# Banded attention ahead of a cosine MLP: value rows of four heads at 192 bytes in a scratch tensor, one load per half batch, for pairs 4 to 7 as well

## Chip, core and metric

One Trainium2 chip, one of its cores. The metric is the device time of one execution in microseconds (us), the median of three runs. All profile times are microseconds from the start of the profiled span unless a number is marked ns.

## What is computed

Attention over 8 batches of 8 heads with 576 positions of width 64, and after it an MLP whose activation is h·cos(h). A query sees keys at most 32 positions away; eight global positions see all and are seen by all.

```python
scores = scale * np.matmul(q, k.transpose(0, 1, 3, 2))
mask = (np.abs(pos[:, None] - pos[None, :]) <= 32) | is_global[:, None] | is_global[None, :]
attn = softmax(np.where(mask, scores, -1e9))
x = np.matmul(attn, v).transpose(0, 2, 1, 3).reshape(4608, 512)
h = x @ w_in            # 512 -> 2048
out = (h * np.cos(h)) @ w_out
```

## The kernel before

**Pieces of work.** The heads are taken in 32 pairs, four pairs to a batch, two pairs to a "half batch" (16 half batches, called s). For one pair the keys are cut into 11 blocks of 56 queries against 120 keys, and the 8 global rows are put in front of each block, so that a block is 128 keys (tile `kw`), 64 queries (tile `qb`) and 128 value rows (tile `vw`). The steps of a pair are:

- `k`, `q` (`local_k` L495, `local_q` L504): fill `kw` and `qb`. For pairs 0 to 7 this is 32 transposes on TensorE (L492) with one copy of `kw` on ScalarE (L499) and two copies of `qb` (L512), from tiles `kn` and `qn` that GpSimd's queue loads with a cast (`load_qk`, L269, step `L`). From pair 8 on, k and q are first cast to scratch tensors `k16` and `q16` in device memory (`cast_half`, L253, steps `K` and, inside the loop, `G`), then read back with a transposing transfer (`turn_half` L272) and copied by VectorE (L502, L515).
- `s` (`scores`, L517): 11 matmuls in three groups, exp on ScalarE (L527), the mask on VectorE (L528).
- `p` (`values`, L531): 22 matmuls with `vw`, then sums, reciprocals and the scaling on VectorE (L542 to L548).
- `x` (`turn_x`, L552): six transposes, two VectorE operations; after the fourth pair of a batch, eight GpSimd copies (L568) that put the global columns in place. They use eight indices that GpSimd reads into registers (`pool_idx`).

**Where value rows come from.** For pairs 0 to 7 (half batches 0 to 3) the values are loaded in natural order by 24 transfers on SyncE's queue (`load_vn`, L334), cast to 16 bits by one ScalarE and two VectorE instructions per half batch (`cast_vn`, L346, step `C`) and moved to the right partitions by matmuls with shift matrices (`spread`, L361, step `w`: 32 matmuls of 128 columns at L370 and L374, then two ScalarE and one VectorE evacuations at L377 per pair). From pair 8 on, v is cast to `v16` (row after row of 64 elements, 128 bytes) and each pair's `vw` is filled from it by two to five transfers on SyncE's queue (`load_v` L305), in pieces of 128 bytes; two more bring the global rows (`load_vg` L379).

**The MLP.** Work goes in tiles of 512 tokens. One unit of the first product is `mlp_in` (four matmuls of 512 columns, L578) with `mlp_act` (sine table on ScalarE L584, product on VectorE L585); one unit of the second product is `mlp_out` (four matmuls, L595; after each fourth, an evacuation and an output transfer, L604). The weights come by GpSimd's queue with a cast: `w_in` in four quarters (`W`, L688), `w_out` in one transfer (`O`, L692).

**The order** is written out by hand. `FRONT` runs all steps of pairs 0 to 7 except the first scores' preparations; `MID`, `FOURTH`, `FIFTH`, `SIXTH` and `ORDER` are the bodies for half batches s = 3, 4, 5, 6 and later ones, in which `1` is a unit of the first product, `2` one of the second, `m` and `t` the matmul part and the activation part of a `1`. Each engine and each queue works its instructions in this order. At the end of a body `bring(s + 2)` (step `B`) turns k and q of the half batch after next and loads its values; in the middle `G` (`casts`) issues the casts of half batch s + 3 on GpSimd's queue. The step `A` (`later_rows`) is 24 small transfers on SyncE's queue for the global rows of batches 4 to 7. The first 20 units of the first product are spread over `FRONT` (2) and `MID` (18); then come the first units `2`, at the start of `FOURTH`.

Of the kernel before, what the change touches and what calls it, by code (L numbers as in the profile page):

```python
# [19 lines left out]
P = 128  # L20
NP = H // 2
# [21 lines left out]
MID = "+ 1 1 kc qc 1 1 kd qd V K6 1 1 1 1 1 1 B5 1 1 n2 1 1 1 1 1 1 -"  # L43

FOURTH = "2 2 sa0 sa1 sa2 2 sz0 2 sz1 sz2 pa 1 1 2 xa pz G 1 1 2 xz n 1 1 2 kc qc 1 kd qd 2 1"
# [5 lines left out]
FRONT = ("s0.0 s0.1 s0.2 k1 q1 C0 w0 s1.0 s1.1 s1.2 L2 p0 k2 q2 C1 w1 x0 s2.0 s2.1 s2.2 W0 p1 k3 q3 C2 w2 x1 "  # L51
         "s3.0 s3.1 s3.2 L3 W1 A g4 g5 p2 k4 q4 w3 x2 s4.0 s4.1 s4.2 g6 g7 c4 K4 W2 W3 p3 k5 q5 C3 w4 x3 s5.0 s5.1 s5.2 p4 k6 q6 w5 x4 n0 "
         "s6.0 s6.1 s6.2 K5 p5 k7 q7 w6 x5 B4 s7.0 s7.1 s7.2 O p6 w7 n1 x6 m p7 m x7 t t")
# [145 lines left out]
def kernel(  # L199
# [38 lines left out]
    v16 = dram.tile([B * H * S, D], FP16)  # L238
# [4 lines left out]
    NV = 4  # L243
    kT = [keep.tile([P, 2, KT], FP16, name=f"kT{i}") for i in range(2)]
    qT = [keep.tile([P, 2, QT], FP16, name=f"qT{i}") for i in range(2)]
    kn = [keep.tile([KP, 2 * 2, RW, D], FP16, name=f"kn{i}") for i in range(2)]
    qn = [keep.tile([QP, 2 * 2, RW, D], FP16, name=f"qn{i}") for i in range(2)]
    vw = [keep.tile([P, NB, 2, D + 1], FP16, name=f"vw{i}") for i in range(NV)]
# [4 lines left out]
    def cast_half(s, which):  # L253

        base = s * 4 * S * D
        for x in which:
            if x == "v":
                nc.gpsimd.dma_start(v16[s * 4 * S : (s + 1) * 4 * S].rearrange("(n r) d -> n (r d)", r=16),
                                    dview(v, base, (16 * D, 4 * S // 16), (1, 16 * D)))
            else:  # L260
                src, dst = {"k": (k, k16), "q": (q, q16)}[x]
                nc.gpsimd.dma_start(dst[s].rearrange("t (h d) -> t h d", h=4),  # L262
                                    dview(src, base, (D, S), (S * D, 4), (1, D)))
# [41 lines left out]
    def load_v(pr):  # L305


        b, h0 = pr // NP, 2 * (pr % NP)
        vt = vw[pr % NV]
        for h in range(2):  # L310
            lo, i0, i1 = (b * H + h0 + h) * S * D, 0, NB
            if pr == 4 * SB and h == 0:
                nc.sync.dma_start(vt[G + 32 : P, 0, h, 0:D], dview(v16, lo, (D, W - 32), (1, D)))
                i0 = 1
# [304 lines left out]
    def weight_squares(c, j):  # L619
        if j == 0:  # L620
            w_sq[c] = work.tile([P, NC, 512], FP16, tag="wsq", bufs=1, name="wsq")
# [243 lines left out]
```

## Time and profile before

| What | Value |
|---|---|
| three runs, us | 366.85, 370.04, 370.23 (median 370.04) |
| profiled execution, us | 371.58, of which the span is 369.8 |
| busy: TensorE, VectorE, ScalarE, GpSimd | 335.9, 266.3, 249.5, 105.9 us |
| TensorE idle in 24.9 to 87.95 us (front and `MID`) | about 10 us |
| TensorE idle in 138 to 282 us | 0 |
| first matmul of the second product (`FOURTH`) | 87.8 us |
| SyncE: the 24 transfers of step `A` | 27.78 to 46.98 us |
| `w_out` issued | 51.68 us |

How to read it: the span falls into a front (to about 72 us), in which attention of pairs 0 to 7 is most of the work and TensorE, VectorE and ScalarE take turns; a middle, in which TensorE never stops; and a tail, in which only the MLP is left. Time that an engine other than TensorE saves in the middle is worth nothing, and time that TensorE spends waiting in the front shifts everything after it.

### The profile page before, as it was taken

How to read it: one execution, taken by the hardware profiler on the slowest of the kernel's cores; microseconds unless marked ns; L12 is line 12 of the kernel's file. 1: busy time of each engine (PE TensorE's matmuls, PEld its weight loads, DVE VectorE, ACT ScalarE, POOL GpSimd, SP SyncE). 2: the span in 40 equal slices, each digit the busy share in tenths (PEclk: the TensorE clock that was granted, in tenths of full speed). 3: DMA queues.
4: the chain of work that ended last, by engine and by line, in shares of the span. 5: the costliest groups of instructions: out<-in, count | busy, mean ns of one | idle time of the engine just before them, and what ended most of it. 6: DMA issues, size and time to landing. Idle time of an engine off the chain costs nothing.

```text
span 369.8 us, 8014 instructions
## 1 busy us (share of the span) xinstructions
PE 335.9 (91%) x2934; PEld 184.9 (50%) x2934; DVE 266.3 (72%) x615; ACT 249.5 (67%) x384; POOL 105.9 (29%) x239
## 2 busy tenths in 40 slices
PE   0399883999998999999999999999999999999992
PEld 0277673545553545555555555555555444444441
DVE  7659974696888888888888888888878445455410
ACT  5488882679776677778777868677787756644300
POOL 6735670161335250705253252603000100000000
PEclk9999997899999999999999999999999999999999
DMA  5979999999999999999999999999920000100111
GB/s 92 197 129 159 180 165 107 198 176 147 102 161 105 194 126 195 125 169 138 195 161 159 160 142 165 160 202 118 130 59 31 28 30 28 57 30 28 53 64 65
DMA packets 176280, 45.57 MB, mean 123 GB/s; under 512 B 164937, under 2 KB 171337, under 8 KB 176041
## 3 DMA queue, kind: packets, MB, share of 16 engines
q1 hardware_dynamic: 112601, 27.61, 58.3%
q0 software_dynamic: 63632, 17.37, 50.3%
q8 instruction: 25, 0.41, 0.5%
q14 instruction: 22, 0.18, 0.2%
HBM read 45.07 MB, written 20.05 MB: 176 GB/s over the span
## 4 chain that ended last, share of the span: by engine, by line
PE 79%; DVE 6%; issue 5%; ACT 3%; POOL 3%; DMA 2%; POOLq 0%; ACTq 0%
PE po L595 32%; PE ph L578 30%; PE st L525 5%; PE pv L537 4%; PE tx L560 2%; PE t L374 2%; DMA qn<-in_q_dram 2%; DVE g L585 2%; ACT e L527 1%; PE t L370 1%; PE t L492 1%; PE pn L628 1%; DVE xn L548 1%; POOL q L262 1%; ACT qb L512 1%
## 5 line engine op out<-in xcount | busy, mean ns | idle before, releaser
L584 ACT ACTIVATE cos<-ph,pio 128x512 f16<-128x512 f32 x144 | 97.1, 687 | 66.3 <-PE ph L578 64.7
L595 PE MATMUL po<-w_out,g 128*128 128x512 f16 x576 | 141.6, 379 | 0.0
L578 PE MATMUL ph<-xT,w_in 128*128 128x512 f16 x576 | 140.1, 379 | 0.3 <-DVE g L585 0.2
L585 DVE TENSOR_TENSOR g<-cos,ph 128x512 f16<-128x512 f16 x144 | 95.9, 685 | 46.9 <-ACT cos L584 44.9
L595 PEld LDWEIGHTS <-g 128*128 128x128 f16 x576 | 55.2, 98 | 62.1
L578 PEld LDWEIGHTS <-w_in 128*128 128x128 f16 x576 | 53.6, 98 | 60.5 <-issue 1.3
L527 ACT ACTIVATE e<-st 128x512 f16<-128x512 f32 (+1 forms) x96 | 47.9, 561 | 15.5 <-PE st L525 9.4
L528 DVE TENSOR_TENSOR pm<-e,mask 128x512 f16<-128x512 f16 (+1 forms) x96 | 37.2, 405 | 22.8 <-ACT e L527 21.0
L752 POOL COPY gate<-xn 1x1 f16<-1x1 f16 x12 | 2.2, 181 | 132.3 <-DVE xn L548 132.3
L525 PE MATMUL st<-qb,kw 128*128 128x128 f16 x352 | 29.2, 223 | 9.4 <-issue 5.0
L525 PEld LDWEIGHTS <-kw 128*128 128x128 f16 x352 | 24.1, 100 | 19.8 <-issue 9.1
L548 DVE TENSOR_TENSOR xn<-pv,r_all 128x768 f16<-128x768 f32 x32 | 30.7, 958 | 1.7
L568 POOL COPY xT<-xg 128x4 f16 x64 | 19.6, 306 | 28.7 <-DVE xT L563 25.3
L262 POOL DMA_DIRECT2D q<-in_q_dram x12 | 26.2, 2181 | 0.0
L614 ACT ACTIVATE sq<-xn 128x1536 f16<-128x1536 f16 x16 | 23.6, 1476 | 0.0
L515 DVE COPY qb<-qT 64x616 f16<-64x616 f16 x48 | 22.1, 460 | 0.3
L374 PE MATMUL t<-xT 112*128 112x128 f16 (+1 forms) x168 | 21.1, 240 | 0.7 <-ACT xT L349 0.4
L600 ACT COPY o<-po 128x512 f32<-128x512 f32 x18 | 10.5, 586 | 15.5 <-PE po L595 15.1
L262 POOL DMA_DIRECT2D k<-in_k_dram x12 | 19.8, 1646 | 0.0
L370 PE MATMUL t<-vg,xT 128*128 128x128 f16 x88 | 18.4, 242 | 0.9 <-issue 0.6
L537 PE MATMUL pv<-vw,pm 128*64 128x65 f16 x704 | 18.5, 199 | 0.0
L602 DVE COPY o<-po 128x512 f32<-128x512 f32 x18 | 12.3, 685 | 6.9 <-PE po L595 6.9
(123 smaller groups left out, 326.8 us busy)
## 6 DMA issues: line engine op xcount, KB each, us to landing
out_dram<-o SPq DMA_DIRECT2D x36, 256.0 KB
vw<-v SPq DMA_DIRECT2D x35, 165.0 KB
v<-in_v_dram POOLq DMA_DIRECT2D x12, 288.0 KB, 4.3
k<-in_k_dram POOLq DMA_DIRECT2D x12, 288.0 KB, 9.2
q<-in_q_dram POOLq DMA_DIRECT2D x12, 288.0 KB, 15.8
vn<-in_v_dram SPq DMA_DIRECT2D x20, 112.0 KB
w_in<-in_moe_w_in_dram POOLq DMA_DIRECT2D x4, 512.0 KB, 12.3
w_out<-in_moe_w_out_dram POOLq DMA_DIRECT2D x1, 2048.0 KB
```

Source lines behind the costliest of these rows:

```text
L262: nc.gpsimd.dma_start(dst[s].rearrange("t (h d) -> t h d", h=4), dview(src, base, (D, S), (S * D, 4), (1, D)))
L374: nc.tensor.matmul(t[:, j - g0], shift[0:m, a], new[0:m, x, h0 : h0 + 2 * D], start=False, stop=(a, x) == parts[-1])
L525: nc.tensor.matmul(st[:, j], kp[:, g0 + j], view(qp[:, :, g0 + j], (NB * C, 2), (1, C)), start=True, stop=True)
L527: nc.scalar.activation(e[:, :n], st[:, :n], AF.Exp, scale=scale)
L528: nc.vector.tensor_tensor(view(pm[:, g0], (1, n * P)), view(e, (1, n * P)), view(mask[:, g0], (1, n * P)), ALU.mult)
L537: nc.tensor.matmul(pv[r0 : r0 + C, j // 6, c0 : c0 + 65], pm[:, j, h], vp[:, j, h], start=True, stop=True)
L548: nc.vector.tensor_tensor(view(xn, (384, 2), (D, 6), (1, D)), view(pv, (512, 2), (65, 6), (1, D)), view(rp, (6, 2), (1, 6), (0, D)), ALU.mult)
L578: nc.tensor.matmul(ph, w_in16[:, j, f * P : (f + 1) * P], xT[:, j, t * TT : (t + 1) * TT], start=(j == 0), stop=(j == NC - 1))
L584: nc.scalar.activation(cos, ph, AF.Sin, bias=pio2)
L585: nc.vector.tensor_tensor(g, cos, ph, ALU.mult)
L595: nc.tensor.matmul(po, g16[:, f, s * P : (s + 1) * P], w_out16[:, f], start=(f == 0), stop=(f == NF - 1))
L614: nc.scalar.activation(sq, view(xn, (1, 2 * BP * P)), AF.Square, accum_out=x_sq[:, s : s + 1])
```

## The change

1. Scratch `v16` becomes two tensors of 768 rows, each row holding four heads at 96 elements (192 bytes) a head: 64 values, a one, and 31 zeros; data starts at row 32. Zeros and ones are put in once, by two memsets on VectorE and two transfers of 590 KB on SyncE's queue (`clear_v16`). `vw` becomes two tiles for a half batch each, with the same layout; a half batch is loaded by one transfer in pieces of 768 bytes (`load_v(s)`).
2. The cast of v writes 64-element pieces into those rows (before: 16 rows to a piece). In `cast_half` v comes last (before: first).
3. Half batches 2 and 3 (pairs 4 to 7) take this way too: no natural loads, no casts `C2`, `C3`, no `w4` to `w7`. Their casts are issued ahead of `FRONT` and at its first steps, their loads (`v2`, `v3`) behind `p1` and `p3`.
4. `FRONT`: `w_in` quarters 0 and 1 move up to just behind the first global copies, 2 and 3 to behind `c3`; the eight index reads of GpSimd (`r`) move from ahead of `FRONT` to behind them; k and q of pair 5 come ahead of the scores of pair 4; `w_out` (`O`) goes ahead of the casts of half batch five (`K5`); eight units of the first product are interleaved with the last steps instead of two, with the third PSUM tag in use from there (`+`). `MID` keeps 12 of 18.
5. The 24 transfers of `A` are split: eight at the start of `MID`, eight at its end, eight behind the first two units of `FOURTH`.
6. Buffers for squares are taken from `qn` and `kn`; that has to do with space only.

```diff
-MID = "+ 1 1 kc qc 1 1 kd qd V K6 1 1 1 1 1 1 B5 1 1 n2 1 1 1 1 1 1 -"
-FOURTH = "2 2 sa0 sa1 sa2 2 sz0 2 ..."
+MID = "A0 1 1 1 1 kc qc 1 1 kd qd V K6 1 1 B5 1 1 n2 1 1 A1 -"
+FOURTH = "2 2 A2 sa0 sa1 sa2 2 sz0 2 ..."
-FRONT = ("s0.0 s0.1 s0.2 k1 q1 C0 w0 s1.0 s1.1 s1.2 L2 p0 k2 q2 C1 w1 x0 s2.0 s2.1 s2.2 W0 p1 k3 q3 C2 w2 x1 "
-         "s3.0 s3.1 s3.2 L3 W1 A g4 g5 p2 k4 q4 w3 x2 s4.0 s4.1 s4.2 g6 g7 c4 K4 W2 W3 p3 k5 q5 C3 w4 x3 s5.0 s5.1 s5.2 p4 k6 q6 w5 x4 n0 "
-         "s6.0 s6.1 s6.2 K5 p5 k7 q7 w6 x5 B4 s7.0 s7.1 s7.2 O p6 w7 n1 x6 m p7 m x7 t t")
+FRONT = ("s0.0 s0.1 s0.2 k1 q1 C0.0 C0.1 C1.0 w0 s1.0 s1.1 s1.2 L2 c3 W2 W3 r p0 k2 q2 C1.1 w1 x0 s2.0 s2.1 s2.2 p1 v2 k3 q3 w2 x1 "
+         "s3.0 s3.1 s3.2 L3 g4 g5 g6 g7 p2 k4 q4 w3 x2 k5 q5 s4.0 s4.1 s4.2 K4 p3 v3 k6 q6 s5.0 s5.1 s5.2 x3 c4 "
+         "p4 k7 q7 s6.0 s6.1 s6.2 x4 n0 O K5 p5 s7.0 s7.1 s7.2 n1 + m m x5 B4 p6 t t m m x6 t t m m p7 t t m m x7 t t")
...
-    v16 = dram.tile([B * H * S, D], FP16)
+    VR = 6 * P
+    VP = D + 32
+    v16 = [dram.tile([VR, 4, VP], FP16, name=f"v16{i}") for i in range(2)]
...
+            src, dst = {"k": (k, k16[s]), "q": (q, q16[s]), "v": (v, v16[s % 2][32 : 32 + S])}[x]
+            dst = dst[:, :, 0:D] if x == "v" else dst.rearrange("t (h d) -> t h d", h=4)
+            nc.gpsimd.dma_start(dst, dview(src, base, (D, S), (S * D, 4), (1, D)))
...
+    def clear_v16():
+        n = VR // P
...
+        nc.vector.memset(vrow, 0.0)
+        nc.vector.memset(view(vrow[:, D : D + 1], (VP, 4 * n)), 1.0)
+        for t in v16:
+            nc.sync.dma_start(t.rearrange("(p n) h d -> p (n h d)", p=P), vrow)
...
+    def load_v(s):
+        r = 4 * VP
+        nc.sync.dma_start(vw[s % NV][G:P].rearrange("p n h d -> p n (h d)"),
+                          dview(v16[s % 2], 0, (r, W), (QB * r, NB), (1, r)))
...
-    SB = 2
+    SB = 1
...
         for pr in range(4):
             globals_k(pr)
             globals_q(pr)
-        pool_idx = [nc.values_load(...) for g in range(G)]
+            if pr == 0:
+                load_w_in(0)
+                load_w_in(1)
...
+        clear_v16()
+        def load_values(s):
+            load_v(s)
+            load_vg(2 * s)
+            load_vg(2 * s + 1)
...
-                    cast_half(n, "vkq")
+                    cast_half(n, "kqv")
...
+        cast_half(2, "v")
```

## Prediction

> **What bounds the kernel now.** I read the page's busy rows first, then busy time by stage, then the chain and the waits, then each engine's timeline from 24 to 90 us. By stage:
>
> ```profile
> core 0: us, PE busy (x) PEld busy (x) DVE busy (x) ACT busy (x) POOL busy (x), PEclk, DMA share, GB/s
> 30.10:35.30 5.20, 4.73 (x105) 4.01 (x103) 5.04 (x14) 4.68 (x9) 3.80 (x9) 1.00 1.17 167
> 57.25:62.29 5.04, 0.00 (x0) 0.00 (x0) 0.75 (x3) 0.00 (x0) 0.00 (x0) 0.85 1.72 86
> 62.29:68.31 6.02, 6.02 (x69) 5.18 (x69) 3.24 (x8) 2.36 (x5) 0.00 (x0) 0.56 1.85 163
> 72.44:87.95 15.51, 15.28 (x71) 6.74 (x69) 13.83 (x26) 12.53 (x20) 8.62 (x24) 1.00 1.66 167
> 138.00:281.90 143.90, 143.90 (x1236) 77.59 (x1234) 122.99 (x281) 110.88 (x163) 42.47 (x100) 1.00 1.44 149
> ```
>
> From 72 us on TensorE hardly stops; in 138 to 282 it is busy all the time, so what other engines or queues save there is worth nothing. In the front a pair takes 5.2 us, of which VectorE works 5.04 and ScalarE 4.68. Then TensorE stands for 5.04 us and works 6.02 us at 0.56 of its clock. Its timeline shows three stops that wait for nothing visible:
>
> ```profile
> 42.32 0.33 PE L492 MATMUL t<-ident,qn 78*64 78x78 f16 x7 [0.96 <-issue]
> ...
> 49.33 0.22 PE L370 MATMUL t<-vg,xT 128*128 128x128 f16 x1 [0.59 <-issue]
> ...
> 62.29 1.01 PE L525 MATMUL st<-qb,kw 128*128 128x128 f16 x8 [5.04 <-issue]
> ```
>
> Counted in the program's order, they lie behind matmuls 475, 603 and 731: exactly 128 apart, 256 instructions with the weight loads. That is instruction fetch. The longest fell while k and q of half batch 4 were being turned and values came in 128-byte pieces:
>
> ```profile
> 50.31 6.17 SPq L275 DMA_TRANSPOSE qT<-q  x1
> 56.66 0.45 SPq L313 DMA_DIRECT2D vw<-v  x1
> 57.29 5.98 SPq L320 DMA_DIRECT2D vw<-v  x2
> ```
>
> The clock to beat is therefore 87.95 us, when the first units `2` are done starting: from there the work of both kernels is the same.
>
> **The change part by part.** All sums are against the profiled execution (371.58 us, span 369.8); it lies 1.5 us above the median of 370.04, so I carry the difference over to the median.
>
> *Spreads of pairs 4 to 7 and casts of half batches 2, 3 removed.* On TensorE `w4` ran from 42.58 to 44.83, 2.25 us; the four take 9.0 at full clock. Evacuations, by L377's rows: ScalarE 4 × (0.59 + 0.48) = 4.3 us, VectorE 4 × 0.69 = 2.8. Casts: VectorE 2 × (0.56 + 0.27) = 1.7, ScalarE 2 × 0.62 = 1.2. VectorE and ScalarE set the front's pace, so a pair falls from 5.2 to about 4.1 us.
>
> *The front added up again.* The scores of pair 4 began at 39.41; their exp at 39.83. Without `C2` ScalarE is 0.6 earlier; pair 5's copies (1.27 + 0.67) now lie ahead: exp at 41.2. VectorE starts on it at 41.9 and then has, for pairs 4 to 7: masks 4 × 1.2, scaling of `p3` to `p5` 3 × 1.55, `qb` 2 × 0.8, `x3` and `x4` 2 × 0.65, together 12.4, to 54.3. ScalarE: exp 4 × 1.48, copies 2 × 1.94, squares 2 × 1.66, 13.1, to 54.3 as well. Then VectorE: `x5` to `x7` 2.0, `p6`, `p7` 3.1, eight products 8 × 0.63 = 5.0, to 64.4. `MID`: 12 products 7.6, a memset 0.2, four copies of pairs 8 and 9 2.7, to 74.9; TensorE's 12 units take 12 × 0.865 = 10.4, much the same. VectorE at 95% of its time (97% in the dense row above): 1.7 us more. The eight units moved from `MID` are in the sum.
>
> *Stops of TensorE.* 128 matmuls apart in the new order they fall behind `p2`, in `p3`, behind `x4` and at the first unit of `MID`; the last two blocks have 7 and 14 us to come in. The 5.04 us and the half clock behind it (6.02 × 0.44 = 2.6 us) go; I leave 0.8 us for stops that reach VectorE (range 0 to 5). By the Trainium skill, "Runtime: NRT & Kernel Launch", Instruction fetch mechanics, instructions come in 16 KiB blocks of 256, mostly hidden. The trace agrees with the 256 and not with hidden, at 5.04 us; if the rule held wholly, that stop had another cause and could stay.
>
> *Scratch and its clearing.* Memsets: the 128×1024 one took 0.91 us; 1152 words, 1.0 + 0.1. VectorE idled 1.5 us ahead of the first mask, so 0; uncovered, 1.1. The transfers: 1.18 MB; outputs alone moved at 303 to 369 GB/s, so 3.5 us, or 5.9 at the 199 GB/s of 70 to 80 us. The cast of v of half batch 2 waits for them on GpSimd's queue, and the loads of k and q (`L2`) stand behind it. GpSimd sat still from 19.85 to 24.91, which I take for the index reads, now moved behind `W3`; so `L2` is issued at 23 to 25 as before (24.91) and has until 35 us.
>
> *DMA.* From 17 us to `w_out` GpSimd's queue carries 2.1 (`w_in`) + 0.6 (v) + 1.2 (k, q) + 0.6 + 0.3 (half batch 4) + 2.1 = 6.9 MB. Before, it carried 7.1 MB from 24.9 to about 79 us, where the rate falls off: 131 GB/s. So 52 us, `w_out` landed at 69, or 73 with the clearing; needed at 77. The loads of v become 1320 pieces of 768 bytes a half batch, not 5200 of 128, which ran at about 52 GB/s in 92 to 96 us. `L3` lands between 41 and 46 by the same sum, wanted at 41.5: 0 to 4.5 us, and I take 0, since its issue is as early as before and the 24 small transfers are out of the way; both ends go to the range. The cast of v in 128-byte pieces costs GpSimd like that of k, 1.1 us from issue to issue instead of 0.5; in the steady stage `gate` waits 132 us in all, so 0. Half batch 5 is short: its copy L502 took 1.62 us, not 0.53, beside GpSimd's issues at 118 us, and TensorE waited 1.35; there I charge 0.5 (0 to 1). By the Trainium skill, "DMA: Bandwidth & Descriptors", Specifications, a piece under 512 bytes is read, changed and written. That speaks for the 768 bytes and against the new cast; the 52 GB/s agrees for reads, and no run here shows the cast.
>
> *GpSimd's queue.* `W0` and `W1` (0.8 us each) go ahead of the global copies of pairs 1 to 3, which ended at 19.9; 21.5 now, and pair 1's scores began at 23.9: 0. With `L2` at 24, `c3`, `W2`, `W3` (4 us) and the index reads (5) end at 33, `L3` follows (31.3 before), then the copies of pairs 4 to 7 (3.9) to 39; pair 4's scores want the first of them at 39: 0 to 1, I take 0. `K4` ends at 42, the eight copies of batch 0's global columns at 50 (behind `x3`), in time for the first `m` near 52. `c4` waits for `v2` to be read out of the same scratch; `w_out`, `K5` and the copies of batch 1 are queued behind it. `v2` is issued behind `p1` at 31 and moves 1.0 MB: landed before 45, so `c4` waits for nothing and `w_out` is issued near 51, as before. In the steady stage the cast of v in `G` waits in the same way for a load that was issued half a body earlier, about 8 us; hidden, and what is queued behind it (the columns' copies) is wanted 8 us later.
>
> *SyncE's queue.* Twelve natural loads fewer, 10 us; v by 14 transfers instead of 73; global rows by 56 instead of 48. `v2` waits there for `p1`, `v3` for `p3` (41); `B4`'s turning stands behind them, for which `K4` has to land anyway (48 to 51; before, it was issued at 48.2). Its copies are wanted in `MID`, near 66. The 24 transfers of `A` took 18.4 us: eight now stand ahead of `B5`, whose k and q are needed 13 us behind `MID`; eight stand ahead of the outputs, which have three buffers. Nothing waits: 0; if an output did, up to 6.2.
>
> *Sum.* First units `2` at 74.9 + 1.7 + 0.8 = 77.4, against 87.95: 10.5 earlier; minus 0.5 in half batch 5: 10.0. Span 359.8, execution 361.6, median 360.0.
>
> **Rivals.**
> A. *The front waits for transfers.* `L3` 4.5 us late, or a stop of 3 to 5 us at 48 us: for it speaks that before, DMA was busy throughout 30 to 52 us and the stops grew; against it, fewer instructions per us. Gain 4 to 6: 364 to 366.
> B. *Slower: `w_out` late.* It has to land before `FOURTH`. If GpSimd's queue ran under 6.9 MB / 71 us = 97 GB/s, it would land behind 88 us and every us later is one lost. At 85 GB/s: 98 us, 10 lost, 380. For it: clearing and two more half batches of values share the engines (+2.0 MB), and 50 to 60 us moved only 118 GB/s in all. Against it: the measured 131 included the 128-byte loads, which are fewer.
> C. *Gain in full.* No stop, VectorE without gaps, as in the dense row: 74.9 and nothing lost in half batch 5, 13 earlier; with `n1` and the table load hidden 2 more: 355 to 357.
> D. *It does nothing:* the front is bound by transfers rather than by VectorE, so that the spreads only filled time. The row 30.10 to 35.30 speaks against it: 366.5 to 373.
>
> **How the numbers follow.** Forecast 0.45 (357 to 363.5), A 0.20, C 0.10, D 0.09, B 0.16. Within 1% of 370.04, about what a measurement of this kernel can tell from no change, is 366.3 to 373.7. Faster: 0.45 + 0.20 + 0.10 = 0.75; same: 0.09; slower: 0.16. Range: leaving out B and part of C, 354 to 368.
>
> **What would show it.** In the new profile: no L370 or L374 of pairs 4 to 7 (44 and 84 instructions instead of 88 and 168); masks of pair 7 ending near 54 us (before 64.4); no stop over 2 us and no clock under 1.0 in 40 to 65; the first `po` near 77 without a wait for DMA; 143.9 us of full TensorE unchanged. I am wrong if TensorE waits at L492 for `kn`, at L537 for `vw`, or at the first L595.

## The result and the profile after

The changed kernel takes 381.48 us in the median (379.8 to 382.79), the kernel before, run beside it, 368.56 (366.85 to 370.23): a ratio of 1.035, 95% interval 1.027 to 1.042. It is slower, by some 13 us, where 10 us less were predicted. The profiled execution took 381.24 us, with a span of 379.5 (before: 371.58 and 369.8). Some executions of a kernel are over 1.5% longer than its fastest; the ratios leave them out and the medians do not, so that a ratio can differ a little from the quotient of the medians.

The same table by stage as for before (span from and to, its length, busy time of each engine, granted clock, DMA share, GB/s):

```profile
core 0: us, PE busy (x) PEld busy (x) DVE busy (x) ACT busy (x) POOL busy (x), PEclk, DMA share, GB/s
41.40:50.97 9.57, 1.25 (x33) 0.92 (x29) 3.30 (x8) 2.78 (x5) 1.57 (x1) 0.65 1.31 207
50.97:58.00 7.03, 6.63 (x117) 6.09 (x118) 3.80 (x10) 4.95 (x8) 1.33 (x7) 0.51 1.55 196
71.00:81.66 10.66, 10.55 (x48) 4.59 (x48) 10.38 (x21) 7.70 (x12) 4.53 (x17) 1.00 1.34 221
99.91:125.14 25.23, 15.18 (x138) 8.47 (x137) 13.59 (x33) 12.84 (x19) 6.41 (x10) 0.89 1.36 145
125.14:133.97 8.83, 6.93 (x51) 3.32 (x50) 4.66 (x13) 3.83 (x7) 3.43 (x10) 0.75 1.12 211
140.00:270.00 130.00, 128.61 (x1058) 68.54 (x1056) 110.92 (x247) 99.49 (x151) 55.15 (x108) 1.00 1.50 172
```

Before, TensorE's longest stop from 72 us on was one of 1.35 us, in half batch 5. Now it works 15.18 of 25.23 us there, and in the front there is a hole of over 8 us; behind both the granted clock is low (0.75 and 0.51 of full speed). TensorE's timeline shows the three stops; in brackets the idle time and what ended it:

```profile
50.97 0.79 PE L495 MATMUL t<-ident,kn 86*64 86x86 f16 x16 [7.62 <-DMA kn<-in_k_dram]
...
124.02 1.33 PE L528 MATMUL st<-qb,kw 128*128 128x128 f16 x11 [9.72 <-issue]
133.97 1.89 PE L581 MATMUL ph<-xT,w_in 128*128 128x512 f16 x8 [1.90 <-POOL xT L571]
```

The first waits for k of pairs 6 and 7 (`L3`); the second, as VectorE's timeline shows, for the turned k of half batch 6 (it is marked `issue`, that is, without a visible cause, but the matmul starts 0.1 us behind the copies of `qb`, which follow that of `kw`); the third for the global columns on GpSimd.

```profile
121.94 0.54 DVE L505 COPY kw<-kT 128x1320 f16<-128x1320 f16 x1 [8.79 <-DMA kT<-k]
122.97 0.95 DVE L518 COPY qb<-qT 64x616 f16<-64x616 f16 x2 [0.49 <-DMA qT<-q]
```

What held up that turning stands ahead of it on SyncE's queue. Both timelines, after and before (its lines are L318 to L320 loads of v, L381 global rows, L604 outputs, L274 and L275 the turning; the half batch is the same):

```profile
91.02 0.54 SPq L320 DMA_DIRECT2D vw<-v  x1
91.62 5.51 SPq L383 DMA_DIRECT2D vw<-vg  x4
97.34 11.16 SPq L777 DMA_DIRECT2D qg<-in_q_dram  x8
108.70 5.64 SPq L777 DMA_DIRECT2D vg<-in_v_dram  x8
114.44 1.00 SPq L607 DMA_DIRECT2D out_dram<-o  x2
115.53 2.72 SPq L273 DMA_TRANSPOSE kT<-k  x1
```

```profile
95.61 2.73 SPq L381 DMA_DIRECT2D vw<-vg  x2
98.44 6.57 SPq L604 DMA_DIRECT2D out_dram<-o  x2
105.11 1.93 SPq L274 DMA_TRANSPOSE kT<-k  x1
```

The 16 row transfers `A1` and `A2` take 16.8 us there, and the turning is issued 10.4 us later than before, in a kernel that entered the half batch 4.8 us earlier. Not all of the 16.8 is their own. The chain of work that ended last goes through the load of v, which is issued at 91.02 and lands at 104.63, and only then through the last 13 of the row transfers:

```profile
91.02 13.61 DMA vw<-v
104.65 0.54 SPq L777
```

At 0.73 us from one to the next the 16 would take 11.7; the other 5 us are mostly this wait. GpSimd's queue shows the other two stops:

```profile
26.30 1.60 POOL L262 DMA_DIRECT2D v<-in_v_dram  x1 [4.78 <-DMA v<-vrow]
27.41 1.22 POOL L268 DMA_DIRECT2D kn<-in_k_dram  x1
...
34.90 0.74 POOL L268 DMA_DIRECT2D kn<-in_k_dram  x1 [2.41 <-PE st L528]
...
130.11 1.59 POOL L262 DMA_DIRECT2D v<-in_v_dram  x1 [16.22 <-DMA vw<-v]
131.19 2.74 POOL L571 COPY xT<-xg 128x4 f16 x8
```

At 26.30 the cast of v waits for the clearing, and the loads of k and q for pairs 4 to 7 wait behind it. At 130.11 a cast of v waits 16 us for the load that still reads its scratch; the columns' copies start right behind it, and TensorE has been waiting for them.

**A yardstick.** There are 36 outputs, in the same order in every version. The time at which the evacuation of the n-th begins says how far a version is ahead or behind (us against before; from the 19th on it hardly changes any more, and equals the difference of the spans within 0.5 us):

| Version | 1st (92.4) | 3rd (109.3) | 6th (137.2) | 17th (227.1) | 19th on |
|---|---|---|---|---|---|
| changed kernel | −4.6 | −4.8 | +8.2 | +8.8 | +9.7 |
| e1_rows_later | −0.9 | −1.0 | +11.3 | +13.8 | +13.8 |
| e2_w_after_l3 | −0.8 | −0.9 | +11.0 | +12.1 | +12.1 |
| e3_both | −0.1 | −0.1 | +11.7 | +14.3 | +16.3 |
| e4_before_rows_split | +2.5 | +2.5 | +3.1 | +3.1 | +3.1 |
| e5_rows_early | +2.7 | +2.5 | +5.3 | +6.4 | +6.5 |
| e6_rows_early_w_late | +1.1 | +0.9 | +0.4 | +0.5 | +3.0 |
| e7_layout_only | +9.8 | +10.4 | +9.9 | +11.3 | +13.2 |
| e8_three_scratch | +3.9 | +4.5 | +4.1 | +7.1 | +7.6 |
| e9_vrows_fifth | +2.4 | +2.4 | +7.8 | +9.1 | +9.0 |
| e10_vrows_fifth_clear_early | −5.7 | −5.9 | +0.7 | +1.3 | +1.3 |
| e11_layout_clear_first | +6.1 | +6.7 | +6.2 | +7.1 | +9.3 |
| e12_rows_in_fifth | −2.2 | −2.4 | +4.5 | +8.1 | +9.2 |
| e13_cast_pieces | −6.3 | −5.6 | −2.7 | +0.7 | +1.3 |
| e14_old_scratch | +1.5 | +1.3 | +13.2 | +14.0 | +14.0 |
| e15_old_scratch_order | +2.1 | +1.9 | +3.4 | +17.1 | +17.1 |
| e16_v_cast_behind_columns | −1.0 | −1.0 | −0.6 | +0.5 | +0.5 |
| e17_global_rows_first | +1.8 | +1.8 | +1.6 | +8.1 | +8.1 |
| e18_half5_held | +2.4 | +2.4 | +1.9 | +6.5 | +6.5 |

The front differs from execution to execution: e10 and e16 have the same front, and their first outputs lie 4.6 us apart, so that less than that between two profiles says nothing about the front. The changed kernel is 4.6 us ahead at the first output (6.1 at the first matmul of the second product, 81.66 against 87.78 us, where 10.5 were predicted) and loses 13.0 between the third and the sixth, in half batch 5: stops of 9.72 and 1.90 us and 2.2 of half clock (8.83 × 0.25), less 1.35 us that the kernel before lost there, are 12.5 of it. Another 1.5 go later.

### The profile page after: what moved, and what is told of

It is laid out like the page before. It is cut to its first block, busy times and chain, and to the rows that moved or that the text cites. A ratio compares the mean times of both kernels' runs of the same rounds, so it can differ in the third digit from the quotient of the medians.

```text
span 379.5 us, 7652 instructions
## 1 busy us (share of the span) xinstructions
PE 332.1 (87%) x2806; PEld 180.2 (47%) x2806; DVE 263.9 (70%) x607; ACT 245.1 (65%) x374; POOL 121.6 (32%) x241
## 4 chain that ended last, share of the span: by engine, by line
PE 56%; DMA 16%; DVE 6%; SPq 5%; issue 5%; POOL 5%; ACT 3%; POOLq 1%; ACTq 0%; DVEq 0%
PE po L598 24%; PE ph L581 24%; DMA vw<-v 9%; DMA qn<-in_q_dram 4%; PE st L528 3%; PE pv L540 2%; DMA v<-vrow 2%; SPq L777 2%; SPq L274 2%; PE tx L563 2%; POOL xT L571 2%; DVE g L588 1%; POOL v L262 1%; SPq L273 1%; PE pn L631 1%
## 5 line engine op out<-in xcount | busy, mean ns | idle before, releaser
L598 PE MATMUL po<-w_out,g 128*128 128x512 f16 x576 | 143.8, 384 | 0.0
L528 PE MATMUL st<-qb,kw 128*128 128x128 f16 x352 | 30.3, 233 | 12.5 <-issue 9.7
L262 POOL DMA_DIRECT2D v<-in_v_dram x14 | 26.8, 1915 | 44.9 <-DMA vw<-v 24.0
L528 PEld LDWEIGHTS <-kw 128*128 128x128 f16 x352 | 25.3, 105 | 22.8 <-issue 13.0
L571 POOL COPY xT<-xg 128x4 f16 x64 | 16.5, 258 | 25.2 <-DVE xT L566 21.8
L617 ACT ACTIVATE qn<-xn 128x1536 f16<-128x1536 f16 x16 | 23.6, 1475 | 0.0
L495 PE MATMUL t<-ident,kn 86*64 86x86 f16 x128 | 5.6, 250 | 17.3 <-DMA kn<-in_k_dram 16.4
L505 DVE COPY kw<-kT 128x1320 f16<-128x1320 f16 x24 | 14.4, 600 | 8.8 <-DMA kT<-k 8.8
## 6 DMA issues: line engine op xcount, KB each, us to landing
w_out<-in_moe_w_out_dram POOLq DMA_DIRECT2D x1, 2048.0 KB, 20.3
```

What stands on the lines that cost most here:

```text
L262: nc.gpsimd.dma_start(dst, dview(src, base, (D, S), (S * D, 4), (1, D)))
L528: nc.tensor.matmul(st[:, j], kp[:, g0 + j], view(qp[:, :, g0 + j], (NB * C, 2), (1, C)), start=True, stop=True)
L571: nc.gpsimd.tensor_copy(xT[:, :, bass.ds(pool_idx[g] + b * S, 1)], xg[:, :, g : g + 1])
L598: nc.tensor.matmul(po, g16[:, f, s * P : (s + 1) * P], w_out16[:, f], start=(f == 0), stop=(f == NF - 1))
L617: nc.scalar.activation(sq, view(xn, (1, 2 * BP * P)), AF.Square, accum_out=x_sq[:, s : s + 1])
```

## The experiments

My theory was the order on the queues: `A` ahead of the turning, `W2` and `W3` ahead of `L3`, the cast of v ahead of the columns. The rival was that the transfers as a whole are too many, so that order only moves the loss. Every number in these paragraphs is the median of the version's runs, with the ratio to the kernel before in the same series, unless it is a time in a profile.

**e1_rows_later: `A1` and `A2` behind the turning of half batch 6.**

```diff
-MID = "A0 1 1 1 1 ... n2 1 1 A1 -"
-FOURTH = "2 2 A2 sa0 ..."   FIFTH = "sa0 ..."      SIXTH = "sa0 ..."
+MID = "A0 1 1 1 1 ... n2 1 1 -"
+FOURTH = "2 2 sa0 ..."      FIFTH = "A1 sa0 ..."   SIXTH = "A2 sa0 ..."
```

> The changed kernel, with the 16 small transfers that stand ahead of the outputs of half batch 4 moved behind the turning of half batch 6: eight at the start of half batch 5, eight at the start of half batch 6. Theory SyncE: the stop of TensorE at 114 to 124 us (9.7 us), the half clock behind it (2.2 us) and the 1.9 us wait for the columns come from SyncE's queue, where the 16 transfers and the load of v of half batch 5, that the fourth of them waits for, held up the turning of k for half batch 6 until 115.5 us. Then this runs at 367 to 370 us, and that turning is issued before 105 us. Rival, transfers as such: the casts and loads of half batches 5 and 6 are too slow for the engines, so k arrives near 121 us whatever stands ahead of it: 379 to 382 us. The front is as in the changed kernel: first unit of the second product at 81.7 us.

385.18 us, ratio 1.043 (1.037 to 1.049). The turning was issued at 104.01 instead of 115.53 and the stop fell from 9.72 to 2.39 us, as the theory says of the place; of the total it was wrong:

```profile
52.80 0.79 PE L495 MATMUL t<-ident,kn 86*64 86x86 f16 x16 [9.86 <-DMA kn<-in_k_dram]
...
120.39 0.77 PE L528 MATMUL st<-qb,kw 128*128 128x128 f16 x11 [2.39 <-issue]
128.19 2.55 PE L581 MATMUL ph<-xT,w_in 128*128 128x512 f16 x8 [2.46 <-POOL xT L571]
149.16 4.71 PE L598 MATMUL po<-w_out,g 128*128 128x512 f16 x12 [6.36 <-ACT o L603]
```

The total also lies above the rival's 379 to 382. The last stop is this edit's own doing: a ScalarE copy in `SIXTH` (step `D2`) reads what `A2` brings. The first shows that the front differs between executions by 2 us and more although nothing in it was changed.

**e2_w_after_l3 and e3_both: `W2 W3` behind `L3`; e3 with e1's edit as well.**

```diff
-s1.2 L2 c3 W2 W3 r p0 ... s3.2 L3 g4 g5
+s1.2 L2 c3 r p0 ... s3.2 L3 W2 W3 g4 g5
```

> The changed kernel, with the two later quarters of w_in issued behind the loads of k and q for pairs 6 and 7 instead of ahead of them. Theory FIFO: those loads (issued at 34.9, landed at 51) stood behind 1.05 MB of w_in on GpSimd's queue; 5 us at 200 GB/s. Then TensorE's 7.6 us wait for k falls to 1 to 3 us, the half clock from 51 to 58 us goes, the first unit of the second product starts at 74 to 77 us instead of 81.7, but the total gains nothing or little (376 to 382 us), because SyncE's queue still sets when k of half batch 6 comes. Rival, all transfers share the engines: the loads come as late as before, since the load of v of half batch 2 and the casts take the bandwidth: wait of 6 us or more.

> Both edits together. If the two losses are separate, the gains add up: 11 to 13 us from SyncE's queue and 5 to 7 us from the front, 361 to 365 us, which is faster than the kernel before (368.6). If the front's gain is eaten by a later wait (w_out, or k of half batch 5), 366 to 370 us.

e2: 385.53, ratio 1.046 (1.039 to 1.052). e3: 387.24, ratio 1.049 (1.042 to 1.055). Both are slower than anything that was expected of them. The wait for `kn` fell from 7.62 to 2.88 us in e2 (1.30 more for `qn`), and a new one came in `MID`, where TensorE waits for a product of VectorE, which had stood behind the copies of the turned q of half batch 4:

```profile
47.51 0.50 PE L495 MATMUL t<-ident,kn 86*64 86x86 f16 x16 [2.88 <-DMA kn<-in_k_dram]
...
81.04 5.80 PE L581 MATMUL ph<-xT,w_in 128*128 128x512 f16 x16 [5.78 <-DVE g L588]
```

In e3 the two edits did not add up: stops of 6.39 (the same place), 3.27 (columns) and 7.17 us (`D2`). The first fits the rival, that order only moves the loss; the last is e1's edit's own doing once more.

**e4_before_rows_split: the kernel before, with only `A` split as in the change.**

```diff
-MID = "+ 1 1 kc qc ... 1 1 -"      FOURTH = "2 2 sa0 ..."     FRONT: "L3 W1 A g4"
+MID = "+ A0 1 1 kc qc ... 1 1 A1 -" FOURTH = "2 2 A2 sa0 ..."  FRONT: "L3 W1 g4"
```

> The kernel before, with nothing but the 24 small transfers split as in the change: eight at the start of the stage between front and loop, eight at its end, eight behind the first two units of the second product. Theory SyncE: the split alone holds up the turning of k for half batch 6 (issued at 105.1 us before) by the 12 us that 16 transfers take: 374 to 381 us. Rival: it needs the single large load of v, that the transfers wait for; with v in many short loads the split costs less than 3 us: 367 to 371 us.

375.19 us, ratio 1.017 (1.010 to 1.025). In the loop nothing was lost here (stop of 1.35 us in half batch 5, as before), although the turning was issued at 114.64. The reason is when it is wanted: TensorE comes to the scores of half batch 6 at 121.62 us here (122.97 less the stop of 1.35) and at 114.30 in the changed kernel (124.02 less 9.72). So a turning issued near 115 costs nothing in e4 and 9.72 us there. The rows were cheaper as well, 11.5 us for 16, since no load of 990 KB stands ahead of them. What grew is the stop that the prediction put down to instruction fetch, at the same matmul:

```profile
65.00 1.01 PE L525 MATMUL st<-qb,kw 128*128 128x128 f16 x8 [7.18 <-issue]
```

**e5_rows_early, e6_rows_early_w_late, e8_three_scratch.** e5 is the changed kernel with `A0 A1` behind the index reads and `A2` behind `v3`, none in `MID` and `FOURTH`; e6 also has `W2 W3` behind `K4`; e8 is e5 with a third scratch tensor.

```diff
-L2 c3 W2 W3 r p0 ... K4 p3 v3 k6          (MID with A0 and A1, FOURTH with A2)
+L2 c3 W2 W3 r A0 A1 p0 ... K4 p3 v3 A2 k6     (e5)
+L2 c3 r A0 A1 p0 ... K4 W2 W3 p3 v3 A2 k6     (e6)
```

> The changed kernel with the 24 small transfers back in the front, in SyncE's gaps: 16 ahead of the first load of v (queue idle from about 23 to 34 us), 8 behind the second (idle from 53 to 58 us). Unlike e1, nothing later waits for them. Theory SyncE: without them SyncE turns k of half batch 6 some 12 us sooner, no stop over 3 us is left in 90 to 200 us, and of the 381.5 us (383 to 385 in the state of e1 and e2) 12 to 15 go: 369 to 373. Rival, front bound by transfers: the small transfers delay the first load of v and the whole front, and what is gained behind is lost there: 376 to 382.

> e5 with the two later quarters of w_in issued behind the casts of k and q of half batch 4, so that neither k and q of pairs 6 and 7 nor those of half batch 4 stand behind them. If e2's front gain (7.6 us of waiting down to 2.9) was lost again only because k of half batch 4 then came late (TensorE stood 5.8 us at 75 to 81 us), this keeps it: 3 to 6 us faster than e5, 364 to 368. If the front is bound by the sum of bytes, another wait takes its place and it is within 2 us of e5.

> e5 with three scratch tensors for v instead of two, so that a cast of v waits for a load one half batch older. Theory: GpSimd's waits at the cast of v for a load (24 us in three waits in the changed kernel) go, and with them TensorE's waits of 1.9 to 2.5 us for the columns' copies behind it: 2 to 4 us faster than e5. Rival: these waits are covered or the third clearing (590 KB) costs as much in the front: within 1.5 us of e5.

e5: 377.65, ratio 1.020 (1.010 to 1.030). e6: 374.46, ratio 1.012 (1.004 to 1.021). e8: 378.68, ratio 1.017 (1.003 to 1.032). Half batch 5 now costs 2.8 us in e5 and nothing in e6 (13.0 in the changed kernel): that loss was SyncE's order. In total the interval of e6 lies clear of the changed kernel's, that of e5 still touches it. But the front gave its gain back:

```profile
83.17 5.01 PE L581 MATMUL ph<-xT,w_in 128*128 128x512 f16 x16 [7.32 <-DVE g L588]
```

This is e6: `A2` now stands ahead of the turning of half batch 4 (issued at 64.09 us; 48.2 before). In e8 the columns' waits of over 1 us were gone, but the front's wait for `kn` was 8.04 us instead of 4.99, and in the loop TensorE now waits some 0.43 us in nearly every half batch for a copy of GpSimd (columns or `kw`), 3.6 us from the sixth output to the 19th. So there is no gain in total. Whether the third clearing made the longer wait for `kn`, or the front's spread, stays open.

**e7_layout_only and e11_layout_clear_first: the kernel before with only the new scratch, its clearing, the one load and the 128-byte cast.** Pairs 4 to 7 stay with the shift matmuls. In e7 my placing of the clearing (step `Z` ahead of `L3`) shared a buffer with the natural loads, was issued at 40.35 us and held `A` up; e11 writes it from another buffer ahead of `FRONT`.

```diff
-s3.0 s3.1 s3.2 L3 W1 A g4      (FRONT, MID and FOURTH of the kernel before)
+s3.0 s3.1 s3.2 Z L3 W1 A0 A1 A2 g4    (e7; Z = clear_v16)
+s3.0 s3.1 s3.2 L3 W1 A0 A1 A2 g4      (e11; clear_v16 ahead of FRONT)
```

> The kernel before with the new scratch layout alone: 192-byte rows of four heads, one load per half batch, clearing, v cast last; pairs 4 to 7 still by spread matmuls, order of the front, small transfers, w_in, w_out and units as before. By the DMA share of the page the layout is neutral: 14 casts in 128-byte pieces cost the 16 engines about 36 us more, the loads in 768-byte pieces about 39 us less. Theory: 367 to 372, so the harm lies in pairs 4 to 7 and in the new order of the queues. Rival: the layout itself (v cast behind a load out of the same scratch, holding GpSimd's queue and the copies behind it; one long load that the eighth transfer after it waits for) costs: 373 to 378.

> As e7_layout_only (order of before, pairs 4 to 7 by shift matmuls, new scratch, one load per half batch, v cast in 128-byte pieces), but the clearing goes ahead of FRONT as in the changed kernel. In e7 it was issued only at 40.35 us and held up the 24 row transfers and the turning of half batch 4 behind it (61.5 us instead of about 48). Theory (the layout is close to neutral, what costs is what stands on the queues behind it): turning issued near 50, no stop over 2 us in MID, total 369 to 374. Rival (the casts into 128-byte pieces and the clearing cost by themselves): 379 or more, as e7.

e7: 383.57, ratio 1.036 (1.026 to 1.047). e11: 381.52, ratio 1.023 (1.007 to 1.039). I had expected e11 to be neutral; it is not, though the turning came in time (51.75). The largest part is one wait:

```profile
91.72 3.60 PE L597 MATMUL po<-w_out,g 128*128 128x512 f16 x8 [4.71 <-DMA w_out<-in_moe_w_out_dram]
```

`w_out` was issued at 57.06, behind the casts of half batches 4 and 5, which take GpSimd longer now, and landed 34.7 us later. That is the prediction's rival B, in a kernel with nothing but the layout.

**e9_vrows_fifth, e10_vrows_fifth_clear_early, e12_rows_in_fifth.** e9 is e6 with `A2` at the start of `FIFTH`; e10 also issues the clearing as the first thing behind the natural loads; e12 is the changed kernel with `A1` at the start and `A2` in the middle of `FIFTH`.

```diff
-K4 W2 W3 p3 v3 A2 k6 q6 ...    FIFTH = "sa0 ..."
+K4 W2 W3 p3 v3 k6 q6 ...       FIFTH = "A2 sa0 ..."
-vrow = work.tile(... tag="g" ...)      clear_v16() ahead of FRONT
+vrow = view(w_out16, ...)              clear_v16() behind the gathers (e10)
```

> As e6_rows_early_w_late, but the last eight row transfers (A2) move from behind v3 to the start of FIFTH. In e6 they took SyncE's queue from 52.66 to 64.09 us, the turning of k of half batch 4 stood behind them (64.09), that of q came at 66.16, and TensorE stood 7.32 us in MID for it. Theory (order on SyncE's queue): the turning is issued near 53, lands near 70, the stop of 7.32 us and the half clock behind it go, about 9 us: span 362 to 366, the first version ahead of the kernel before. Rival (the transfers as a whole are too many, and order only moves the loss): a stop of 4 us or more shows up at another place, the columns' 2.4 us stay, total within 2 us of e6's 374.5.

> As e9, and the clearing of the scratch (memsets into the space of w_out instead of a buffer of g) comes ahead of the mask's preparation: issued near 12.5 us, as soon as the natural loads leave a slot, not at 18.3. Theory (GpSimd's queue waits for the clearing, 6.79 us in e6, and everything queued there, c2, k and q of pairs 4 to 7, K4, comes late by it): that wait goes down to 1 us or less, the loads of pairs 4 and 5 come 5 us earlier and the front's waits of 1.4 and 1.5 us go: 2 to 4 us below e9. Rival (those waits only trade places with VectorE's pace, and the clearing disturbs the first loads instead): within 1 us of e9 or slower, with a later first matmul of the scores.

> The changed kernel, with the last 16 row transfers moved behind the turning of half batch 6: A1 from the end of MID to the start of FIFTH, A2 from FOURTH to the middle of FIFTH (not to SIXTH as in e1, where a ScalarE copy then waited for them). In the changed kernel outputs 4 to 6 fall behind by 13 us against before. Theory (SyncE's queue holds up the turning of half batch 6): under 3 us lost between outputs 3 and 6, total 371 to 374. Rival (another wait takes the place, as in e1): 378 or more.

e9: 380.04, ratio 1.017 (1.001 to 1.033): a miss. The stop in `MID` fell to 3.79, and 4.87 us for `w_out` and 2.88 for `vw` took its place, the rival's forecast. e10: 373.23, ratio 1.013 (1.006 to 1.020). The 5.79 us that GpSimd waited for the clearing in e9 are gone, and the first output is 8.1 us earlier (3.5 in e16, which has e10's front). In total the two can't be told apart: their intervals overlap. e10 still waits 5.31 us for `vw` in the front (at 59.97 us); what it lost in the loop, 7.1 us, lay mostly in half batch 5:

```profile
115.92 0.77 PE L527 MATMUL st<-qb,kw 128*128 128x128 f16 x11 [2.70 <-issue]
125.09 3.19 PE L580 MATMUL ph<-xT,w_in 128*128 128x512 f16 x8 [3.79 <-POOL xT L570]
```

e12: 380.66, ratio 1.024 (1.013 to 1.035). The stop of 9.72 us fell to 2.71, but two half batches lost another 2.2 and 1.6 us to columns and scores (6.9 us between outputs 3 and 6, where under 3 were expected), and the front had an 8.10 us wait for `kn`. The total is not clear of the changed kernel's 1.035 (1.027 to 1.042).

**e13_cast_pieces and e14_old_scratch, e15_old_scratch_order.** e13 is the kernel before, with the cast of v alone in 128-byte pieces. e14 is the changed kernel with scratch, casts and loads of v of the kernel before; e15 the same with the order of e9.

```diff
-v16[...].rearrange("(n r) d -> n (r d)", r=16)
+v16[...].rearrange("(h t) d -> t h d", h=4)      (e13)
```

> The kernel before, in which the cast of v alone is changed: the same scratch and the same loads, but written in pieces of 64 elements (128 bytes), position by position over the four heads, not 16 rows to a piece. In the changed kernel such a cast took 9.9 us to land in the median, before 4.3 us. If these pieces cost by themselves (GpSimd's time to issue, 1.1 us more per cast, and the time on the shared engines): 373 to 380, with a later turning of half batch 4 or w_out later than 88 us. If they cost nothing and it is the load of 990 KB or the clearing: within 2 us of before (367 to 371).

> The changed kernel with the scratch, the vw tiles, the casts and the loads of v of the kernel before (no clearing, own rows for every half batch, 128-byte loads): order, the eight units, pairs 4 to 7 by way of the scratch, w_out ahead of half batch five and the split row transfers stay as changed. If the layout is what costs: no wait of GpSimd for clearing or scratch, L3 issued near 30 and not 34.9, no columns' waits; the front ends 4 us or more earlier than in the changed kernel (first output 8 us or more ahead of before), total 370 to 375 with only the loss of half batch 5 left. If the order costs: within 2 us of 381.5, with the same 8 us lost between outputs 3 and 6.

> As e14, with the order of e9: A0 and A1 behind the index reads, A2 at the start of FIFTH, the third and fourth quarter of w_in behind K4. If layout and queues' order together were the loss: first output 6 to 10 us ahead of before, at most 3 us given back in half batch 5, total 361 to 367, ahead of the kernel before. If transfers as a whole bound the front (rival): 370 or more, with waits of TensorE for vw, w_out or k and q of half batch 4.

e13: 374.70, ratio 1.013 (1.001 to 1.025): the pieces alone cost some 1.3%, only just clear of nothing. In its profile the front is ahead, because the stop of 5.04 us did not come at all, and the loop gives 7.6 us back; at half batch 5 GpSimd took 1.66 us for the cast ahead of the columns' copies, and TensorE waited 2.60 for them (1.35 before). From there to the end of the casts every half batch gives back another 0.65 us, with one such line in each, where the kernel before has none:

```profile
170.44 0.77 PE L525 MATMUL st<-qb,kw 128*128 128x128 f16 x11 [0.49 <-POOL kw L479]
```

So in the loop the 128-byte pieces cost by way of GpSimd's queue: the cast of v takes longer to issue, and the copies behind it come later.

e14: 384.49, ratio 1.041 (1.033 to 1.050). Without the new layout the changed order loses as much, and in the same place:

```profile
71.38 0.22 PE L544 MATMUL pv<-vw,pm 128*64 128x65 f16 x1 [8.97 <-DMA vw<-vg]
...
132.18 1.33 PE L532 MATMUL st<-qb,kw 128*128 128x128 f16 x11 [11.79 <-issue]
```

So the loss of half batch 5 does not need the new layout (here the turning is issued at 122.38 and wanted at 120.39), and values of pairs 4 to 7 by way of the old scratch come too late: change 3 needs change 1. e15: 381.06 (373.82 to 388.35; there is no interval for it, and its profiled execution is the one of 388.35). In that profile the stop moved with `A2`, to half batch 7 (9.68 us at 150.94, the turning of k issued at 137.10 behind eight rows and two outputs).

**e16_v_cast_behind_columns: e10, with the cast of v issued behind the columns' copies.**

```diff
-pz G 1 1 2 xz n        (G casts k, q and v)
+pz G 1 1 2 xz H n      (G casts k and q, H casts v)
```

> As e10 (clearing early, rows split between front and FIFTH), but inside the loop the cast of v is issued behind the columns' copies, not in front of them. If the columns waited for GpSimd's queue, in which the cast of v waited for the load out of the same scratch: the stops of 3.79 us near 125 and the smaller one near 165 go, and GpSimd's copies of the columns start within 1 us of the last pair's product; total 367 to 370, about 4 us below e10. If something else holds the columns up, or v then comes late for its half batch: within 1 us of e10's 373, with waits at the products with vw.

367.67 us, ratio 0.996 (0.991 to 1.001): 5.6 below e10, as the queue theory said, and about 14 below the changed kernel. It is the best version, and level with the kernel before, not ahead of it. In half batch 5 it waits 1.80 us for the columns, where e10 waited 2.70 and 3.79. These are the front's stops in its profiled execution, which took 372.16:

```profile
74.79 5.23 PE L580 MATMUL ph<-xT,w_in 128*128 128x512 f16 x16 [5.91 <-DVE g L587]
85.21 3.41 PE L597 MATMUL po<-w_out,g 128*128 128x512 f16 x8 [5.19 <-DMA w_out<-in_moe_w_out_dram]
```

**e17_global_rows_first and e18_half5_held.** e17 is e16 with the global rows ahead of the load of v; e18 adds a GpSimd copy that should hold back the casts of half batch 5.

```diff
-load_v(s); load_vg(2 * s); load_vg(2 * s + 1)
+load_vg(2 * s); load_vg(2 * s + 1); load_v(s)     (e17)
-n0 O K5 p5
+n0 O p5 h2 K5                                     (e18)
```

> As e16, but within load_values the four small loads of global rows are issued ahead of the 990 KB load of v, not behind it. In e10 and e16 these four took SyncE's queue 8.3 and 4.9 us behind v3 (and 11.2 and 7.1 us behind the load of half batch 4), with the turning of half batch 4 behind them at 52.8 and 47.4 us. If the load in flight holds SyncE's queue up: four issues take under 3 us each time, the turning is issued near 45, its copies no longer hold MID up (stop of 5.9 us down to 2 or less): 362 to 366, ahead of before. If the turning is late because its transfers share the engines (rival): issues as long as before, or the turning lands no earlier; within 1.5 us of e16's 367.7.

> As e17, and the casts of k, q and v of half batch 5, which GpSimd issued right behind w_out at 53 to 56 us, wait for the product of pair 4 or 5 (near 62 us). If w_out is late because these casts share the engines with it: w_out lands within 22 us of its issue (27.3 in e10, 32.9 in e16), no stop for it at the first unit of the second product, 2 to 5 us below e17. If not, or if half batch 5 is then late itself (its turning behind 88 us, a stop at its first scores): level with e17 or slower.

e17: 377.73, ratio 1.022 (1.016 to 1.029). e18: 375.43, ratio 1.012 (1.005 to 1.019). Both miss. SyncE's queue in e16, on which e17 is built, and in e17:

```profile
41.87 0.34 SPq L319 DMA_DIRECT2D vw<-v  x1
42.25 4.86 SPq L382 DMA_DIRECT2D vw<-vg  x4
47.42 5.56 SPq L273 DMA_TRANSPOSE kT<-k  x1
56.81 4.25 SPq L274 DMA_TRANSPOSE qT<-q  x1
```

```profile
39.41 3.26 SPq L382 DMA_DIRECT2D vw<-vg  x4
42.76 0.51 SPq L319 DMA_DIRECT2D vw<-v  x1
45.00 10.24 SPq L273 DMA_TRANSPOSE kT<-k  x1
55.34 7.50 SPq L274 DMA_TRANSPOSE qT<-q  x1
```

The four small loads go out in 3.26 us ahead of the large one, behind it in 4.86 (8.26 in e10), and the turning is issued 2.4 us earlier (7.8 against e10). Then its own issue takes 10.24 instead of 5.56 us, and the turned q is there no sooner: VectorE copies it at 74.56 us, in e16 at 73.07. So in the front the time seems to be that of the transfers, not SyncE's. It is the smaller part of e17's loss, though: between outputs 6 and 8, in the loop, e17 loses 6.6 us and e16 1.1. There the load of v for half batch 7 now stands behind the four small ones. It is issued at 137.87 us (132.67 in e16), and TensorE waits for it, with a clock of 0.50 in the 4 us behind:

```profile
148.00 0.82 PE L539 MATMUL pv<-vw,pm 128*64 128x65 f16 x22 [3.69 <-DMA vw<-v]
```

e18 has the same stop, 3.00 us at 147.65. In e18 the hold was of no use: its copy ran at 54.22 us and the casts followed at 54.48, so whether `w_out` (34.9 us to land) suffers from them wasn't told apart.

## Why the prediction was wrong

**What was right.** TensorE's work of the spreads went, VectorE's pace as well: the masks of pair 7 began at 61.93 us and took 1.02; without the stop of 7.62 and the 3.4 us that half clock cost over the next 7.03, they would by this estimate have ended at 52, and 54 was predicted. The dense stretch at the end of `MID` works as summed up: TensorE is busy 10.55 of 10.66 us. The stop of 5.04 us is gone, and the stops without a visible cause fell where the prediction put the first two of them, behind `p2` (0.87 us at 36.69) and in `p3` (0.71 us at 43.04). `w_out` landed at 80.5 (60.2 + 20.3), just before its first use at 81.66; rival B did not decide this kernel, as it did e11.

**"*SyncE's queue.* ... Nothing waits: 0; if an output did, up to 6.2."** This is the step that failed most: +13.0 us between outputs 3 and 6 instead of 0. I looked at what `A1` and `A2` stand ahead of and saw `B5` and the outputs, and left out what stands behind the outputs, the turning of half batch 6. In e5, e6 and e16, with `A` elsewhere, 2.8, −0.5 and 0.4 us are lost there; in e14, with the old layout, 11.9. The price was mis-sized too: 16 transfers took 16.8 us here, some 5 of it the wait for the load of v (11.5 in e4). e4 sets a limit: in the kernel before, the same split cost the loop almost nothing, since TensorE asks for that k 7.3 us later there. So what the late turning costs hangs on when a kernel gets there: here it took the front's lead of 4.8 us and 8.2 more.

**"`L3` lands between 41 and 46 ..., wanted at 41.5: 0 to 4.5 us, and I take 0, since its issue is as early as before."** This is the second step that failed, and the prediction named its sign, a wait of TensorE for `kn`. `L3` was issued at 34.90 (33 by the sum, 31.3 before), landed 16 us later, and cost 7.62 us and 3.4 of half clock. Two terms stood behind it: "so 3.5 us, or 5.9" for the clearing (8.65 us, 17.35 to 26.0, and `L2` issued at 27.41 instead of 24.91), and `W2`, `W3` and the index reads ahead of it. In e2, with `W2` and `W3` behind it, `L3` was issued no earlier (36.51) but its k was there 11 us later, not 16: what these two cost was the landing. Against e9, the early clearing of e10 and e16 brings the first output forward by 3.5 to 8.1 us; of the total nothing clear of noise.

**"In the steady stage the cast of v in `G` waits in the same way ... hidden".** It waited 16.22 us at 130, and the columns behind it were late. e16 against e10: 5.6 us. The cast was mis-sized as well, by its landing: 9.9 us in the median, 4.3 before, 7.0 in e13 with the pieces alone. And its longer issue, put at 0 because `gate` waits 132 us in all, costs 0.65 us a half batch in e13.

**"*DMA.* ... 52 us, `w_out` landed at 69".** I added up GpSimd's queue alone, and took its bytes at the rate of before. I take this to be why the repaired versions do not reach 360; no run shows it. All queues together, 24 to 90 us, of before, after and e16 (packets, MB; then the software queue that GpSimd feeds):

```profile
DMA packets 30934, 10.17 MB, mean 154 GB/s; under 512 B 25629, under 2 KB 30877, under 8 KB 30877
q0 software_dynamic: 19609, 8.01, 109.2%
```

```profile
DMA packets 35968, 12.24 MB, mean 186 GB/s; under 512 B 27122, under 2 KB 35846, under 8 KB 35960
q0 software_dynamic: 27762, 7.74, 113.2%
```

```profile
DMA packets 34832, 11.61 MB, mean 176 GB/s; under 512 B 26103, under 2 KB 34822, under 8 KB 34822
q0 software_dynamic: 26529, 7.58, 120.3%
```

By the page's DMA row the engines were busy nine tenths or more in every slice from 28 us to the tail, before the change as well. But that share counts packets that overlap (1.46 in this stretch, before and after alike), and 186 GB/s is more than 154, so it does not show that no room was left. The change adds 2.07 MB there, 13 us at the 154 GB/s of before, 11 at the 186 of after: as much as the front was to save, which may be chance. And GpSimd's queue moves its bytes in 42% more packets, since v is written in 128-byte pieces, and five casts of it fall into this stretch instead of three. By the Trainium skill, "DMA: Bandwidth & Descriptors", Specifications, a piece under 512 bytes costs a read and a write back; the landing in e13 (7.0 instead of 4.3 us) agrees in sign, while what e13 lost in its loop came by GpSimd's queue. The prediction cited this rule against the cast and then charged the cast nothing in its sum.

**What is shown and what is not.** Shown by undoing: the order of `A` (half batch 5 in e5 and e6, the total in e6), the cast of v ahead of the columns (e16), the cost of the layout by itself (e11, e13, both only just clear of noise); for the front alone, the place of the clearing (e10, e16). Argued, not shown: that the total of transfers is what holds the front. For it speaks that each repair in the front brought out another late transfer (`kn`, q of half batch 4, `vw`, `w_out` in e2, e6, e9, e10, e17), and that an earlier issue did not land earlier (the turned q in e17). Against it speaks that after the change more bytes were moved per us than before, and that e17's loss was for the larger part one of order again. Rival D ("the front is bound by transfers rather than by VectorE") comes nearest to this, and rival A named the late `L3`, with 4.5 us; I let the row 30.10 to 35.30 speak against D, although the same rows gave a DMA share of 1.17 to 1.85: VectorE paced the front, and there was no room behind it.

## What to carry to other kernels

When transfers are moved on a queue, follow the queue to the next item that an engine waits for, past the ones named first, and do it on every queue that the move touches. A wait that a cast or a clearing takes on an in-order queue is paid by everything behind it; put such a step behind what is wanted sooner. Where the DMA engines are busy most of the time anyway, count the bytes and packets that a change adds on all queues: here they may have cost what the saved compute was worth, which is argued and not shown. And ask when a late transfer is wanted, not only when it is issued: the same lateness was free in one kernel and cost 9.72 us in another.

## What the hardware showed unexpectedly

- The stop at the 731st matmul, put down to instruction fetch, was 5.04 us before and 7.18 in e4, and in e13, where program and order on TensorE are the same, no stop over 0.67 us lies between 55 and 90 us. What differs between these kernels is the transfers; how they make or hide the stop isn't shown. In e13 the first output came 6.3 us earlier.
- Where such stops lie goes with the count of instructions. In the trace of the kernel before, the one at 42.32 us lies behind 476 recorded matmuls; in those of the changed kernel, e2, e10, e14 and e15, in which another matmul stands at that place, a stop of 0.71 to 1.81 us marked `issue` lies behind 476 as well.
- Four loads of 11 KB took SyncE 3.1 to 11.2 us to issue in the front when they stood behind a load of 990 KB (e10, e16), and 3.3 to 4.6 us ahead of it (e17).
- TensorE's clock was 0.51 for 7.03 us behind the stop of 7.62 us. By the Trainium skill, "TensorE: Matmul & The Clock Gate", HAM oscillation, gaps over some 3.4 us do this; the trace agrees in that, but a gap need not be that long. By the mean clock of short windows (taking it as either full or half) it fell 0.9 us into this stop (43.35 to 45.00: 0.77, then 0.50), 5.0 us into that of 9.72 (117 to 120: 0.89, then 0.50), and in e17 1.2 us into one of 1.44 (43.60 to 45.04: 0.91, then 0.50).
